# Linear attention and gated MLP on one core: one more tile pair of V as a Strassen group, and exps queued one product later

## The chip, the cores and the metric

One core of one Trainium2 chip runs the whole kernel. The metric is device time in microseconds; below, "us". The same program is run several times, and one further execution is recorded by the hardware profiler. All times inside the kernel are counted from the start of the profiled span.

## The reference

The input x has 2048 tokens of 1024 features, in bf16. Two blocks follow each other:

```
h  = x + A(layernorm(x))            # linear attention, 32 heads of 32
h2 = h + B(layernorm(h))            # gated MLP with 3584 hidden features

A:  q, k, v = split(x @ wqkv)
    phi(t) = where(t > 0, t + 1, exp(t)) + 1e-6
    kv = sum over tokens of phi(k) v ;  z = sum over tokens of phi(k)
    o  = phi(q) kv / (phi(q) z + 1e-6) ;  return o @ wo
B:  gate = x @ W_gate ; up = x @ W_up
    return (relu(gate) * up) @ W_down
```

The change concerns block A alone: the products that make k, v and q, the function phi, and the sum kv.

## The kernel before, in words

The 2048 tokens are 16 tiles of 128 ("st" 0 to 15). A tile is loaded, normalised by VectorE (DVE) with statistics from DVE (`ln1_stats`, L630 to L640) or from ScalarE (`ln1_stats_act`, L654 and L659, which ends on GpSimd, POOL), and turned over into `xnT`: the first four by TensorE (PE), the others by a DMA transpose that SP issues (`T1d`, L526). SP's queue is one list; behind each transpose stands the load of a later tile.

The instructions of all engines are written down in one order by the program, and each engine keeps its own part of that order. A planner adds the waits: an instruction waits for the last writer of what it reads, and for the readers of what it writes. So the place of a call in the source decides what stands ahead of it on its engine.

Two tiles form a pair p. The products of a pair with wk, wv or wq are made by `sgroup` (L833) in a form of Strassen's method, with seven products in place of eight. Each product is four matmuls of 512 columns. The order in a group, with the copies and additions between, is:

| step on PE | then |
|---|---|
| P1 into bank a | ACT copies a to bank b (fk1, L621) |
| P7 into bank f | ACT copies f to a buffer (s7, L621) |
| P6 onto b | ACT copies b to bank c (fk2, L621) |
| P2 onto a | a is the first result, "11" |
| P5 onto c | ACT copies c to a buffer (sc, L621); DVE adds f to it: result "22" |
| P4 onto b | DVE adds b to s7: result "21" |
| P3 onto c | c is the last result, "12" |

P6 needs fk1, P5 needs fk2, and P3, which writes c, needs sc to have read it. The buffer of sc is a single one, `btmp[0]`; s7 alternates between two (`atmp` and `btmp[1]`). The results 22 and 21 stand in these two buffers until they are used.

For k and q each result goes through phi: an exp on ACT (L684), and two instructions on DVE, a minimum and an addition (L688) and the final maximum (L691). I call the two "fin", the last alone "phi", and write exp22 and phi22 for those of result 22. The exp of 11 is issued in its own group. Those of 22, 21 and 12 are put into the table `pend` and issued in the next group (for q groups exp12 in its own); `hook(i)` issues what `pend[i]` holds and what the caller has asked for at that place. hook(1) comes after fk1, hook(2) after s7, hook(3) after fk2, hook(4) after P2 and its exp, hook(5) after sc and the addition, hook(6) after P4, hook(7) at the end.

For v the results are only copied: 11 and 12 by ACT (L970), 21 and 22 by DVE's addition (L964).

The order of the first stage: the v products of tiles 0 to 5 are plain, those of tiles 0 to 3 ahead of all groups (`v_piece`, eight matmuls for half of a tile, copied by ACT at L789); then the group k0, the pieces of v for tiles 4 and 5, and the groups k1, v3, k2, v4, k3, v5, k4, v6, k5, v7, k6, k7, and eight q groups, q0 to q3 (r = 0) and q4 to q7 (r = 1). `kvaccs(p)` adds a pair of tiles into kv with 16 small matmuls of 129 columns, eight for a tile. In the v groups it stands between P4 and P3 (hook 6). It first uses the even tile (results 11 and 12 of the k group), then the odd one (21, then 22). In q4 to q7 the same place holds `a2_num`, and DVE has the division `a2_div` besides (L1053, L1056, L1058).

`x_sums(p)` (L825, four DVE instructions) makes the sums of x that a group of pair p needs; they are used for k, v and q alike. `twk`, `twv` and `twq` are lists of DVE instructions that make the sums of the weights (L800); each pop issues one. `norms(p)` normalises the two tiles of pair p and issues their transposes. The k and v groups and q0 to q3 draw on five PSUM banks, q4 to q7 on four (`A_POOL`), the oldest first. After q7 comes the output product with wo (`a4_mm`, and `a4_h`, L1082), and then block B, which the change leaves alone.

Of the kernel before, what the change touches and what calls it, by code (L numbers as in the profile page):

```python
# [132 lines left out]
def bass_sequential_preLN__linear_attn_block__glu_gated_reglu__prompt_kernel(  # L133
# [64 lines left out]
    with es:  # L198
# [137 lines left out]
        def bank(b, w=512):  # L336
            return ps[:, b, 0:w]
# [375 lines left out]
        def ln1_stats(st):  # L713
            i = st % NX1
            ln1_k[st] = ln_stats(x1[:, i, :], B_x1[i], "ln1_%d" % st)
# [55 lines left out]
        def v_piece(st, h, mid=None):  # L771
            b = alloc_bank(P1_POOL)
            nt = ND2 + h
            for dc in range(NDC):
                if mid is not None and dc == NDC // 2:
                    mid()
                mm(bank(b, NW), xnT[:, dc, st * P:(st + 1) * P], wkv[:, dc, nt * NW:(nt + 1) * NW],
                   dc == 0, dc == NDC - 1, [xnT_buf(st, dc), B_wkv[nt][0 if dc < WKH else 1]], B_bank[b],
                   "v_%d_%d" % (st, h))
            v_copy(b, st, h)  # L780
# [32 lines left out]
        def x_sums(p):  # L813
            def xb(k, t):
                st = 2 * p + t
                return xnT[:, k * KH:(k + 1) * KH, st * P:(st + 1) * P]

            def s(i):
                return Sx(i)[:, :, p * P:(p + 1) * P]

            def bx(k, t):
                return [B_xnT[2 * p + t][k]]

            def add(i, in0, in1, op, reads):
                PL.add("dve", lambda e: e.tensor_tensor(out=s(i), in0=in0, in1=in1, op=op), reads=reads,  # L825
                       writes=[B_Sx[i][p]], name="Sx%d_%d" % (i + 1, p))

            add(2, xb(0, 0), xb(0, 1), ALU.subtract, bx(0, 0) + bx(0, 1))
            add(0, xb(0, 1), xb(1, 1), ALU.add, bx(0, 1) + bx(1, 1))
            add(1, s(0), xb(0, 0), ALU.subtract, [B_Sx[0][p]] + bx(0, 0))  # L830
            add(3, xb(1, 0), s(1), ALU.subtract, [B_Sx[1][p]] + bx(1, 0))

        def sgroup(pool, tok_major, X, SX, W, TW, e11, e12, e21, e22, name, hooks=(), isq=False):  # L833

            hooks = dict(hooks)

            def prod(b, x, w, start, nm):
                (xf, xr), (wf, wr) = x, w
                for kk in range(KH):
                    xa, wa = xf(kk), wf(kk)  # L840
                    l, r = (xa, wa) if tok_major else (wa, xa)
                    o = bank(b)
                    if len(r.shape) == 3:
                        o = o.rearrange("p (a b) -> p a b", b=r.shape[2])
                    mm(o, l, r, start and kk == 0, kk == KH - 1, xr + wr, B_bank[b], name + nm, skip=True)

            def hook(i):
                for f_ in pend.pop(i, ()):
                    f_()
                if i in hooks:  # L850
                    hooks[i]()

            a = alloc_bank(pool)
            f = alloc_bank(pool)
            b = alloc_bank(pool)
            prod(a, X(0, 0), W(0, 0), True, "P1")
            ident_act(bank(b), bank(a), [B_bank[a]], [B_bank[b]], name + "fk1")
            hook(1)
            prod(f, SX(2), TW(2), True, "P7")
            grp[0] += 1  # L860
            s7, b7 = [(atmp, B_at), (btmp[:, 1, :], B_bt[1])][grp[0] % 2]
            sc, bc = btmp[:, 0, :], B_bt[0]
            ident_act(s7, bank(f), [B_bank[f]], [b7], name + "s7")
            hook(2)
            c = alloc_bank(pool)
            prod(b, SX(1), TW(1), False, "P6")
            ident_act(bank(c), bank(b), [B_bank[b]], [B_bank[c]], name + "fk2")
            hook(3)
            prod(a, X(1, 0), W(1, 0), False, "P2")
            for f_ in e11(bank(a), B_bank[a]):  # L870
                f_()
            hook(4)
            prod(c, SX(0), TW(0), False, "P5")
            ident_act(sc, bank(c), [B_bank[c]], [bc], name + "sc")
            s22 = e22(bank(f), B_bank[f], sc, bc)
            s22[0]()
            hook(5)
            prod(b, X(1, 1), TW(3), False, "P4")
            s21 = e21(bank(b), B_bank[b], s7, b7)
            s21[0]()  # L880
            hook(6)
            prod(c, SX(3), W(1, 1), False, "P3")
            s12 = list(e12(bank(c), B_bank[c]))
            if isq:
                s12.pop(0)()
            pend[1] = s12
            pend[2] = list(s22[1:])
            pend[3] = list(s21[1:])
            hook(7)

        pend = {}
# [50 lines left out]
        def k_group(p, hooks=()):  # L942
            X, SX = x_ops(p)
            W, TW = w_ops(wkv, bw_k, tw_k, B_TWk)

            def dst(t, h):
                st = 2 * p + t
                return pk_ap(st)[:, h * NW:(h + 1) * NW], B_pk[pk_slot(st)][h]

            def pl(t, h):  # L950
                d, db = dst(t, h)
                return lambda b, bb: phi_steps(b, bb, d, db, "k_%d_%d" % (2 * p + t, h))
            sgroup(P1_POOL, True, X, SX, W, TW, pl(0, 0), pl(0, 1),
                   add_phi(*dst(1, 0), "k_%d_0" % (2 * p + 1)),
                   add_phi(*dst(1, 1), "k_%d_1" % (2 * p + 1)), "k%d" % p, hooks)
# [470 lines left out]
        twv = w_sums(wv_, bw_v, tw_v, B_TWv, "TWv", KH)  # L1426
# [10 lines left out]
        m5()  # L1437
        twk.pop(0)()
        v_piece(3, 0)
        q5()  # L1440
        ln1_stats(4)
        twk.pop(0)()
        v_piece(1, 1)
        ln1_norm(4)
# [7 lines left out]
        q6()  # L1452
        twv.pop(0)()
        twk.pop(0)()
        twv.pop(0)()
        v_piece(3, 1)
        for i in range(2):
            load_wq(i)
        NP_ = NST // 2

        def kv_hooks(p, nq):

            sq = []
            A, B = 2 * p + 6, 2 * p + 7

            def k1():
                if p > 0 and A < NST:
                    ln1_stats(A)
                for _ in range(nq[0]):
                    twq.pop(0)()  # L1470

            def k5():
                if B < NST:
                    m_, q_ = ln1_stats_act(B)
                    m_()
                    sq.append(q_)

            def k6():
                for f_ in sq:
                    f_()  # L1480
                if 3 <= p + 2 < NP_:
                    x_sums(p + 2)
            return {1: k1, 5: k5, 6: k6}

        def norms(p):
            for st in (2 * p, 2 * p + 1):
                if st < NST:
                    ln1_norm(st)
                    T1d(st)

        def kvaccs(p):
            kvacc(2 * p)
            kvacc(2 * p + 1)

        k_group(0, kv_hooks(0, (0, 0)))
        def run_pend(i):
            for f_ in pend.pop(i, ()):
                f_()

        v_piece(4, 0, lambda: run_pend(1))  # L1500
        run_pend(2)
        v_piece(4, 1, lambda: run_pend(3))
        x_sums(1)
        v_piece(5, 0)
        norms(3)
        twv.pop(0)()
        v_piece(5, 1)
        x_sums(2)
        kvaccs(0)
        NQ = {2: (0, 1), 3: (0, 1), 4: (0, 1), 5: (2, 2), 6: (1, 0)}  # L1510
        for p in range(1, NP_):
            nq = NQ.get(p, (0, 0))
            hooks = kv_hooks(p, nq)
            if p == NP_ - 1:
                hooks[5] = lambda h5=hooks[5]: (h5(), kvaccs(NP_ - 2))
            k_group(p, hooks)
            if p + 2 < NP_:
                def v6(p=p, nq=nq):
                    norms(p + 3)
                    kvaccs(p)  # L1520
                    for _ in range(nq[1]):
                        twq.pop(0)()
                v_group(p + 2, {6: v6})
# [4 lines left out]
        for r in range(2):  # L1528
            for ct in range(NG // 2):
                hooks = {}  # L1530
                if r == 0 and ct == 0:
                    hooks[6] = lambda: kvaccs(NP_ - 1)
                if r == 0 and ct == 2:
                    hooks[6] = kvfin
                if r == 1:
                    hooks[6] = lambda t=ct: a2_num(t)
                q_group(r, ct, hooks)
                if r == 1:
                    pend[1].insert(1 if ct + 1 < NG // 2 else 0, lambda t=ct: a2_div(t))
                if r == 0 and ct == 0:  # L1540
                    for i in range(TPP + NX2):
                        load_x2(i)
# [105 lines left out]
```

## Time and profile before

| | |
|---|---|
| median of 3 runs | 748.24 us (748.11 to 748.42) |
| profiled execution | 747.75 us |
| its span, first to last instruction | 746.0 us |
| granted TensorE clock | 0.999 |
| busy, PE / DVE / ACT / POOL | 736.1 / 536.7 / 309.7 / 43.9 us |
| PE's weight loads | 336.0 us |
| DMA moved | 113.38 MB |

The profiled execution took 1.75 us more than its span, and is 0.49 us under the median. A line of the timeline gives the start and the length of an instruction (or of several alike, "x4"), its engine, its line in the kernel, what it writes and reads, and in brackets the idle time of the engine just before it with what ended it. "PE" are matmuls and "PEld" the weight loads that go ahead of them; a weight load that is the first after a wait starts together with its matmul, others some 0.2 us earlier. The changed code runs between 9 and about 180 us. By stretches, the busy times of the engines are:

| stretch, us | PE | DVE | ACT |
|---|---|---|---|
| 24.0 to 37.3 (k0, v pieces) | 13.25 | 10.97 | 9.26 |
| 37.3 to 112.0 (k and v groups) | 73.88 | 59.49 | 49.08 |
| 112.0 to 145.0 (k7, q0 to q3) | 32.67 | 25.32 | 21.61 |
| 145.0 to 171.6 (q4 to q7) | 26.60 | 24.51 | 17.62 |

### The profile page before, as it was taken

To read this page: it belongs to the slowest core of one execution; us is meant where nothing else is said; L and a number is where in the kernel's file an instruction comes from. 1 tells how busy PE (TensorE), PEld (TensorE's weight loads), DVE (VectorE), ACT (ScalarE), POOL (GpSimd) and SP (SyncE) were. 2 spreads that over 40 slices of the span, in tenths; PEclk is the share of its full clock that TensorE was granted. 3 is DMA by queue.
4 is the path that set the end of the run, shared out by engine and by line. 5 is a ranking of instruction groups with operands and counts; after the bars stand their busy time and mean duration, and the time that the engine had idled before them with its cause. 6 is when DMAs were issued, how large, how long until landed. Compare 5 with 4: busy or idle time off the path is not lost.

```text
span 746.0 us, 10031 instructions
## 1 busy us (share of the span) xinstructions
PE 736.1 (99%) x3539; PEld 336.0 (45%) x3595; DVE 536.7 (72%) x1071; ACT 309.7 (42%) x536; POOL 43.9 (6%) x90
## 2 busy tenths in 40 slices
PE   9999999999999999999999999999999999999998
PEld 4444444344554444444444444444444444444443
DVE  7788866898775899787877585766867677563343
ACT  4767656665832354544543100035444454520000
POOL 2411000001350000000000010000000000000000
PEclk9999999999999999999999999999999999999999
DMA  9642144023998797666428899742324242036764
GB/s 305 202 103 68 35 135 156 1 29 84 230 223 248 222 278 210 179 176 171 142 85 253 231 254 305 240 121 77 110 61 112 58 113 56 1 85 184 211 189 135
DMA packets 160226, 113.38 MB, mean 152 GB/s; under 512 B 51505, under 2 KB 141361, under 8 KB 160177
## 3 DMA queue, kind: packets, MB, share of 16 engines
q1 hardware_dynamic: 160176, 112.75, 54.1%
q8 instruction: 28, 0.46, 0.3%
q14 instruction: 22, 0.17, 0.1%
HBM read 85.46 MB, written 15.73 MB: 136 GB/s over the span
## 4 chain that ended last, share of the span: by engine, by line
PE 88%; DVE 5%; ACT 4%; issue 2%; DMA 0%; SPq 0%; DVEq 0%; POOL 0%; ACTq 0%; POOLq 0%
PE ps L616 88%; DVE RAB L691 1%; ACT ps L621 1%; ACT RX L684 1%; DVE RE L1058 1%; DVE RX L688 1%; ACT RXH L654 1%; ACT RXH L659 1%; ACT RX L621 1%; DVE RX L903 0%; DMA RW<-in_B_W_down_dram 0%; SPq L522 0%; DVE RXH L1082 0%; PE ps L748 0%; DVE RE L691 0%
## 5 line engine op out<-in xcount | busy, mean ns | idle before, releaser
L621 ACT ACTIVATE ps<-ps 128x512 f32<-128x512 f32 x154 | 89.8, 584 | 180.2 <-PE ps L616 161.5
L616 PE MATMUL ps<-RC,RO 128*128 128x512 f16 x672 | 154.4, 379 | 0.5 <-DVE RE L1239 0.4
L616 PE MATMUL ps<-RW,RAB 128*128 128x512 f16 (+1 forms) x681 | 150.1, 379 | 0.6
L616 PEld LDWEIGHTS ps<-RW,RAB 128*128 128x128 bf16 (+1 forms) x692 | 67.7, 98 | 81.6
L616 PE MATMUL ps<-RH,RWG 128*128 128x512 bf16 x435 | 103.2, 379 | 1.0 <-DVE RAB L1232 0.3
L621 ACT ACTIVATE RE<-ps 128x512 f32<-128x512 f32 x120 | 70.8, 597 | 75.3 <-PE ps L616 52.8
L616 PEld LDWEIGHTS ps<-RC,RO 128*128 128x128 f16 x672 | 65.5, 98 | 80.5 <-ACT ps L621 1.1
L616 PE MATMUL ps<-RC,RWG 128*128 128x512 f16 x320 | 76.6, 379 | 0.1
L616 PEld LDWEIGHTS ps<-RH,RWG 128*128 128x128 bf16 x448 | 43.8, 98 | 53.4 <-DVE RAB L1232 0.8
L1232 DVE TENSOR_TENSOR RAB<-ps,RAB 128x512 bf16<-128x512 f32 x28 | 19.3, 690 | 63.6 <-PE ps L616 63.6
L621 ACT ACTIVATE RAB<-ps 128x512 bf16<-128x512 f32 x56 | 33.4, 597 | 61.9 <-PE ps L616 61.8
L616 PE MATMUL ps<-RH,RO 128*128 128x512 bf16 (+1 forms) x242 | 58.3, 379 | 0.7
L616 PE MATMUL ps<-RW,RE 128*128 128x512 bf16 x248 | 56.8, 379 | 0.8 <-DVE RXH L1082 0.4
L616 PE MATMUL ps<-RAB 128*128 128x512 bf16 x196 | 47.7, 379 | 0.3
L616 PEld LDWEIGHTS ps<-RC,RWG 128*128 128x128 bf16 (+1 forms) x320 | 30.0, 98 | 39.9 <-ACT ps L621 5.9
L1163 DVE TENSOR_TENSOR RO<-RWG,RO 128x512 f16<-128x512 bf16 x108 | 45.4, 420 | 1.8
L1163 DVE TENSOR_TENSOR RO<-RWG 128x512 f16<-128x512 bf16 x108 | 40.7, 418 | 3.2 <-DMA RWG<-in_B_W_up_dram 1.6
L1239 DVE TENSOR_TENSOR RE<-ps,RE 128x512 f32<-128x512 f32 x56 | 38.3, 690 | 4.9 <-ACT RE L621 4.9
L1244 DVE TENSOR_TENSOR RE<-ps,RE 128x512 f32<-128x512 f32 x56 | 38.1, 681 | 0.0
L616 PEld LDWEIGHTS ps<-RH,RO 128*128 128x128 f16 (+1 forms) x256 | 24.6, 98 | 29.4 <-ACT RX L621 1.1
L616 PEld LDWEIGHTS ps<-RW,RE 128*128 128x128 bf16 x256 | 24.5, 98 | 27.9 <-DVE RXH L1082 0.7
L688 DVE TENSOR_SCALAR RX<-RX 128x512 bf16<-128x512 bf16 x64 | 18.6, 290 | 22.8 <-ACT RX L684 22.7
(118 smaller groups left out, 764.8 us busy)
## 6 DMA issues: line engine op xcount, KB each, us to landing
RWG<-in_B_W_gate_dram SPq DMA_DIRECT2D x28, 512.0 KB, 4.0
RWG<-in_B_W_up_dram SPq DMA_DIRECT2D x28, 512.0 KB, 5.1
RW<-t_scr SPq DMA_DIRECT2D x56, 256.0 KB, 3.3
RW<-in_B_W_down_dram SPq DMA_DIRECT2D x42, 256.0 KB, 4.0
RW<-in_B_W_down_dram SPq DMA_DIRECT2D x14, 512.0 KB, 4.1
t_scr<-RW SPq DMA_DIRECT2D x14, 512.0 KB, 5.0
RE<-in_A_x_dram SPq DMA_DIRECT2D x23, 256.0 KB, 3.2
RAB<-in_A_wqkv_dram SPq DMA_DIRECT2D x8, 512.0 KB, 8.0
```

Source lines behind the costliest of these rows:

```text
L616: lambda e: e.matmul(out_ap, lhsT, rhs, start=start, stop=stop, skip_group_check=skip),
L621: PL.add("act", lambda e: e.activation(out=dst, in_=src, func=func), reads=reads, writes=writes, name=name)
L654: PL.add("act", lambda e: e.activation(out=junk, in_=src, func=ACTF.Identity, scale=1.0 / D, accum_out=sv[:, 0:1]), reads=src_bufs, writes ...
L659: PL.add("act", lambda e: e.activation(out=junk, in_=src, func=ACTF.Square, scale=float(D) ** -0.5, accum_out=sv[:, 1:2]), reads=src_bufs, ...
L684: PL.add("act", lambda e: e.activation(out=Et[:, k, :], in_=src, func=ACTF.Exp), reads=[src_buf], writes=[B_E[k]], name=name + "_exp")
L688: PL.add("dve", lambda e: e.tensor_scalar(out=Et[:, k, :], in0=Et[:, k, :], scalar1=1.0, scalar2=1e-6, op0=ALU.min, op1=ALU.add), reads=[] ...
L691: PL.add("dve", lambda e: e.scalar_tensor_tensor(out=dst_ap, in0=src, scalar=C1, in1=Et[:, k, :], op0=ALU.add, op1=ALU.max), reads=[src_bu ...
L1058: PL.add("dve", lambda e: e.tensor_tensor(out=osb[:, k, :].rearrange("p (g h e) -> p g h e", h=HPG, e=Dh), in0=nv[:, :, 0:P].rearrange("p ...
L1163: PL.add(eng, lambda e: e.tensor_tensor(out=Tring[:, k, j], in0=in0, in1=in1, op=ALU.subtract), reads=reads, writes=[B_T[k][j]], name="T%d ...
L1232: PL.add("dve", lambda e: e.tensor_tensor(out=hh[:, f1, 0:SBW], in0=bank(BA[1]), in1=r11[:, rr, :], op=ALU.mult), reads=[B_bank[BA[1]], B_ ...
L1239: PL.add("dve", lambda e, w=w: e.tensor_tensor(out=ftmp[:, 4 + w, :], in0=bank(BF_[w]), in1=ftmp[:, 2 + w, :], op=ALU.add), reads=[B_bank[ ...
L1244: PL.add("dve", lambda e, w=w: e.tensor_tensor(out=ftmp[:, 6 + w, :], in0=bank(BB[w]), in1=ftmp[:, w, :], op=ALU.add), reads=[B_bank[BB[w] ...
```

## The change

It does four things. The v products of tiles 4 and 5 (pair 2) are made by a group, v2, instead of four plain pieces. For that the loop over pairs starts at 0, `x_sums(2)` moves into k0 (hook 6), `x_sums(1)` and `norms(3)` into v2, and the last of the `twv` instructions ahead of k0. In every group that has exps pending from the group before, exp22 with its fin goes from hook(2) to hook(3), so behind fk2, and exp21 with its fin from hook(3) to hook(4), so behind P2 and exp11. The sums kv of the pairs 6 and 7 go to the end of k7 (from the place behind P5) and to the end of q0 (from the place behind P4). And the DVE statistics of tile 4, with the POOL instruction that ends them, go ahead of `q5()`, the second half of the ACT statistics of tile 5. Since there is one group more, s7 of each later group uses the other of its two buffers.

```diff
@@ sgroup
             pend[1] = s12
-            pend[2] = list(s22[1:])
-            pend[3] = list(s21[1:])
+            pend[3] = list(s22[1:])
+            pend[4] = list(s21[1:])
             hook(7)
@@ first stage
         v_piece(3, 0)
+        ln1_stats(4)
         q5()
-        ln1_stats(4)
         twk.pop(0)()
...
         twv.pop(0)()
+        twv.pop(0)()
         v_piece(3, 1)
@@ kv_hooks
-                if 3 <= p + 2 < NP_:
+                if p + 2 < NP_:
                     x_sums(p + 2)
@@ loop over pairs
-        k_group(0, kv_hooks(0, (0, 0)))
-        def run_pend(i):
-            for f_ in pend.pop(i, ()):
-                f_()
-
-        v_piece(4, 0, lambda: run_pend(1))
-        run_pend(2)
-        v_piece(4, 1, lambda: run_pend(3))
-        x_sums(1)
-        v_piece(5, 0)
-        norms(3)
-        twv.pop(0)()
-        v_piece(5, 1)
-        x_sums(2)
-        kvaccs(0)
         NQ = {2: (0, 1), 3: (0, 1), 4: (0, 1), 5: (2, 2), 6: (1, 0)}
-        for p in range(1, NP_):
+        for p in range(NP_):
             nq = NQ.get(p, (0, 0))
             hooks = kv_hooks(p, nq)
             if p == NP_ - 1:
-                hooks[5] = lambda h5=hooks[5]: (h5(), kvaccs(NP_ - 2))
+                hooks[7] = lambda: kvaccs(NP_ - 2)
             k_group(p, hooks)
             if p + 2 < NP_:
                 def v6(p=p, nq=nq):
+                    if p == 0:
+                        x_sums(1)
                     norms(p + 3)
                     kvaccs(p)
@@ q groups
                 if r == 0 and ct == 0:
-                    hooks[6] = lambda: kvaccs(NP_ - 1)
+                    hooks[7] = lambda: kvaccs(NP_ - 1)
```

## The prediction

> **What bounds the kernel now.** I read first the page's busy times and chain, then the waits of PE's weight loads, then the timeline of single groups between 23 and 172 us, where the changed code runs.
>
> ```profile
> PE 88%; DVE 5%; ACT 4%; issue 2%; DMA 0%; SPq 0%; DVEq 0%; POOL 0%; ACTq 0%; POOLq 0%
> ```
> ```profile
> PEld ps L616 <- ACT ps L621: 18.8, 44, 0.7
> PEld ps L616 <- ACT RX L621: 3.7, 10, 0.4
> ```
>
> TensorE bounds the kernel, so only what shortens or delays its stream counts. Its weight loads wait mostly for copies on ACT: "ps L621" is fk1 or fk2, "RX L621" is sc. Most of such a wait is normal: a load that runs ahead shows idle too. So I measure by starts of products (four matmuls each). Unhindered ones follow at 0.865 us (P1 to P7 at 70.64 and 71.50), hence 0.216 us a matmul and 6.06 us a group of 28.
>
> The group q1, in the timeline (start, duration, engine):
>
> ```profile
> 128.04 0.60 ACT L621 ACTIVATE RX<-ps 128x512 f32<-128x512 f32 x1 [0.28 <-PE ps L616]
> 128.54 0.62 ACT L684 ACTIVATE RX<-RX 128x512 bf16<-128x512 f32 x1
> 129.06 0.59 ACT L621 ACTIVATE ps<-ps 128x512 f32<-128x512 f32 x1
> 129.52 0.69 DVE L691 SCALAR_TENSOR_TENSOR RAB<-RX 128x512 bf16<-128x512 f32 x1
> 129.57 0.61 ACT L684 ACTIVATE RX<-RXH 128x512 bf16<-128x512 f32 x1
> 129.70 0.55 PEld L616 LDWEIGHTS ps<-RWG,RH 128*128 128x128 f16 x4 [0.48 <-ACT ps L621]
> 130.09 0.59 ACT L684 ACTIVATE RX<-ps 128x512 bf16<-128x512 f32 x1
> 130.82 0.60 ACT L621 ACTIVATE RX<-ps 128x512 f32<-128x512 f32 x1 [0.15 <-issue]
> 131.47 0.55 PEld L616 LDWEIGHTS ps<-RH,RO 128*128 128x128 bf16 x4 [0.37 <-ACT RX L621]
> ```
>
> On ACT stand s7, exp22 of the group before, fk2, exp21, this group's exp11, sc. P5's load at 129.70 waited for fk2. P6 had started at 127.82, and results can be read 1.04+0.09 us after such a start (sc starts at 130.82 after P5 at 129.70), so fk2 could have run at 128.95; exp22 held it 0.11 us. In the k groups, where no exps are pending, P5 starts 1.77 us after P6 (66.20 to 67.97); here 1.88, in v4 2.00 (72.46 to 74.46). So the exps cost about **0.12 us in each of q1 to q7 and 0.23 in v3 to v7, k7 and q0**.
>
> [...] fk2 followed exp22 0.52 us after its start, though its data were there. [...]
>
> **The change, part by part.**
>
> *v pieces to a group.* From the first piece of tile 4 (29.49) to k1 (37.34) PE takes 7.85 us: 32 matmuls (6.92) and kvacc. A v group with kvacc takes 7.36 (v4 at 70.64 to k3 at 78.00). So **-0.49**; four matmuls fewer are 0.86, and 0.37 comes back as the group's waits. ACT gets six copies for four and DVE two additions, inside those 7.36.
>
> *The fourth twv earlier, ln1_stats(4) before q5().* The twv is one 1.22 us addition on DVE. DVE had waited 1.64 us at 21.67 for POOL's rstd of tile 4, which stood behind q5's POOL work; moved ahead, it is ready by about 19.5, and tile 5's norm starts near 21.07 instead of 22.13. The 1.06 won pays for the twv (1.13 start to start): DVE is free at 27.3 as before, when exp11 of k0 ends at 27.66. Both transposes issue some 1.6 us earlier on SP. **0**; without that cover at most +1.1.
>
> *x_sums(1) and norms(3).* DVE now does, in v2, phi21, two additions, x_sums(1) (1.67), then the norms of tiles 6 and 7. From v4's row moved by 41.15 us, x_sums(1) starts near 36.95 and norm 6 ends at 39.17; before it ended at 36.57. SP issues transpose, x load, transpose: the second is 1.91 us after the first (36.59 to 38.50), so at 41.1, and transposes land 3.1 to 3.7 us after issue: 44.4. x_sums(3) in k1 wants it at 37.03 + 6.50 = 43.53 (k2 started at 64.45, its x_sums at 70.95). P7 of v3 then starts near 44.9 instead of 44.1: **+0.8** (0 to 1.2). Later pairs have 6.5 us from issue to use and keep their slack.
>
> *exps one product later.* The copies fk2 gain the 0.12 and 0.23 above. But exp22, fin22 and exp21, fin21 all move, and three things stand behind them:
>
> (a) **sc waits for phi22.** sc writes btmp[0], which phi22 of the group before still reads. exp22's start to phi22's end takes 1.67 us (128.54 to 130.21). In q1 fk2 goes to 128.95, exp22 to 129.46, phi22 ends at 131.13. P5 (now 129.59, 0.64 after fk2) would let sc start at 130.72; exp11 and exp21 on ACT hold it to 130.99, phi22 to 131.16. P3 follows 0.65 later: 131.81 instead of 131.47. **+0.34 in q1, q2, q3 = +1.02.** q0 loses its cover too, as kvaccs(7) moves behind P3: P5 0.23 earlier, P3 0.49 held: **+0.26**. In k7 kvaccs(6), which had stalled 0.26 us for phi21, moves to the end: P3 held to 116.95, next group at 118.76 against 118.77: **0**.
>
> (b) **kvacc waits for phi21 in the v groups.** Its second eight matmuls need it:
>
> ```profile
> 74.33 0.62 ACT L684 ACTIVATE RX<-RXH 128x512 bf16<-128x512 f32 x1
> 75.31 0.69 DVE L691 SCALAR_TENSOR_TENSOR RE<-RXH,RX 128x512 bf16<-128x512 f32 x1
> 75.99 1.13 PEld L616 LDWEIGHTS ps<-RE 128*128 128x128 bf16 x16
> ```
>
> phi21 ended at 76.00; kvacc began on PE at 76.20 and takes 0.94 us (124.26 to 125.20 in q0), so its second half began at 76.67. Afterwards, exp22 starts at 74.10, the v copy at 74.61, exp21 at 75.11; phi22 ends at 75.77 and phi21 at 76.80. PE, 0.23 earlier, wants it at 76.44: 0.41 of wait. **+0.18 in each of six v groups = +1.08.** sc itself is covered by kvacc there.
>
> (c) **DVE is full in q5 to q7.** One fin12 to the next is 6.71 us (159.25 to 165.96) without a gap: four fins 0.93 each, a2_div 1.75, two additions 1.25.
>
> ```profile
> 160.79 1.22 DVE L1058 TENSOR_TENSOR RE<-ps,rden 128x1024 bf16<-128x1024 f32 x1
> 161.93 0.28 DVE L688 TENSOR_SCALAR RX<-RX 128x512 bf16<-128x512 bf16 x1
> 162.86 0.29 DVE L688 TENSOR_SCALAR RX<-RX 128x512 bf16<-128x512 bf16 x1
> 163.79 0.28 DVE L688 TENSOR_SCALAR RX<-RX 128x512 bf16<-128x512 bf16 x1
> ```
>
> With only four banks fk1 writes the bank that the last addition (add21) reads. From the end of add21: fk1 +0.03, P6 +0.65, fk2 +1.13, exp22 +0.51, fin22 +0.64: 2.96 us, in which DVE has 0.93 + 1.75 = 2.68 of work. Then three fins and the additions, 4.06: a period of 7.02. Starting with q4's late phi22, P3 of q7 is 0.72 late and DVE's additions 1.37. The output stage begins DVE-bound: a4_mm(2) at 180.24 waited 0.39 for a4_h(0). So DVE's lateness counts: **+1.37**, of which PE's own is 0.72 (0 if DVE finds its gaps elsewhere).
>
> s7's buffers change parity with one group more, and both alternate on: 0. Bytes, SP's order and later stages stay; those are PE-paced, so the delay stays to the end.
>
> **Sum:** -0.49 + 0.8 + 1.02 + 0.26 + 1.08 + 1.37 = **+4.0 us**. The profiled execution took 747.75 (span 746.0, 1.75 around it) and would become 751.8; the median, 748.24, lies 0.49 above it: I say **752.2**.
>
> **Rivals.**
>
> 1. *Faster: the waits go and nothing takes their place.* Gains: 5 x 0.23 + 2 x 0.23 + 7 x 0.12 = 2.45, with the 0.49: 745.3. For it: the 0.48 waits are plain in the rows. It decides at one place: if phi22 ends before P5's result can be copied. In q1 it is 131.13 against 130.72, so the 1.67 us would have to shrink by 0.41; nothing shortens it, and ACT alone (exp11, exp21) already holds sc by 0.27. 12%.
>
> 2. *Smaller loss.* The transposes land in time and q4 to q7 don't build up: 4.0 - 0.8 - 1.37 = +1.9, 750.1. Against it: DVE's rows are gapless. Its lower half, if kvacc's wait is milder too (-1.1), is no change. 18%.
>
> 3. *Heavier.* fk1 of one group and sc of the next feed each other in r = 0 too, and the transposes land at 44.8: +6, 754.2. 8%.
>
> 4. *My case*: 62%, 750.7 to 753.5. That the change doesn't move the exps is out: the instruction order of the changed kernel has fk2 ahead of exp22 and sc behind exp21, waiting on DVE.
>
> A measurement of this kernel tells about 0.2%, 1.5 us. Faster is rival 1, 0.12; same is the lower part of rival 2, 0.08; slower 0.80. The range, 748.6 to 754.0, leaves out rival 1 and the upper part of rival 3.
>
> **What would show it.** Right: P5 1.77 us after P6 in v and q groups; in q1 to q3 P3 over 2.1 us after P5, its load waiting for ACT RX, sc for DVE; kvacc in two runs of eight; q5 to q7 some 7.0 us apart; P7 of v3 waiting for DVE. Wrong: P3 1.77 after P5 in q1 to q3, or q groups under 6.25 us; then rival 1 holds.

## The result: 753.51 us against 748.17, and the profile after

The changed kernel takes 753.51 us (median, 753.23 to 753.82), the kernel before 748.17 in the same measurement: a ratio of 1.0071 with an interval of 1.0054 to 1.0089. It is slower, by 5.3 us where +4.0 was predicted; the profiled execution took 753.38 us (span 751.6). The chain of the changed kernel, and what its weight loads waited for between 23 and 178 us (us in total, times, longest):

```profile
PE 82%; DVE 9%; ACT 3%; issue 3%; DMA 2%; SPq 1%; POOL 0%; DVEq 0%; ACTq 0%
```
```profile
PEld ps L616 <- ACT ps L621: 16.0, 41, 0.7
PEld ps L616 <- ACT RX L621: 6.6, 12, 0.8
PEld ps L616 <- DVE RWG L825: 4.4, 6, 1.5
PEld ps L616 <- DVE RE L691: 2.4, 6, 0.4
PEld ps L616 <- DVE RX L903: 1.7, 4, 0.4
```

The kernel before, over the same stretch (sc, 3.7 us, as in the prediction's lines):

```profile
PEld ps L616 <- ACT ps L621: 17.8, 42, 0.6
PEld ps L616 <- DVE RWG L825: 1.4, 5, 0.3
PEld ps L616 <- DVE RE L691: 0.3, 1, 0.3
```

The copies fk1 and fk2 ("ps L621") are waited for less, 16.0 us where the kernel before had 17.8. Everything below has grown: sc ("RX L621") from 3.7, the sums of x (L825) from 1.4, phi21 (L691, into RE) from 0.3, and DVE's addition add21 (L903) is new. One wait was exchanged for four.

The group q1 of the changed kernel, in the timeline (start, duration, engine):

```profile
131.79 0.58 ACT L621 ACTIVATE ps<-ps 128x512 f32<-128x512 f32 x1 [0.31 <-PE ps L616]
132.28 0.62 ACT L684 ACTIVATE RX<-RX 128x512 bf16<-128x512 f32 x1
132.42 0.55 PEld L616 LDWEIGHTS ps<-RWG,RH 128*128 128x128 f16 x4 [0.36 <-ACT ps L621]
132.80 0.59 ACT L684 ACTIVATE RX<-ps 128x512 bf16<-128x512 f32 x1
133.26 0.69 DVE L691 SCALAR_TENSOR_TENSOR RAB<-RX 128x512 bf16<-128x512 f32 x1
133.28 0.63 ACT L684 ACTIVATE RX<-RX 128x512 bf16<-128x512 f32 x1
133.99 0.60 ACT L621 ACTIVATE RX<-ps 128x512 f32<-128x512 f32 x1
134.64 0.33 PEld L616 LDWEIGHTS ps<-RH,RO 128*128 128x128 bf16 x3 [0.81 <-ACT RX L621]
```

fk2 (131.79) now goes ahead of exp22 (132.28), and P5 starts at 132.42, 1.77 us after P6 at 130.65: the gain is there. Then ACT has exp11 (132.80) and exp21 (133.28), phi22 ends on DVE at 133.95, and only then sc runs, at 133.99; P3 starts at 134.64, 2.22 us after P5 instead of 1.77.

The profiled execution adds up as follows. Groups are taken from start of P1 to start of P1 of the next; "predicted" joins the terms of the prediction that fall into a group.

| stretch | before | after | measured | predicted |
|---|---|---|---|---|
| start, until v of pair 2 | 29.49 | 29.13 | -0.36 | 0 |
| v of pair 2 (pieces, v2) | 7.85 | 8.17 | +0.32 | -0.49 + 0.18 |
| v3 | 7.36 | 8.65 | +1.29 | +0.8 + 0.18 |
| v5 | 7.36 | 8.15 | +0.79 | +0.18 |
| v4, v6, v7 | 7.36, 7.36, 7.28 | 7.54, 7.54, 7.46 | +0.54 | +0.54 |
| k7, q0 to q3 | 33.77 | 34.98 | +1.21 | +1.28 |
| q4 to q7 | 6.71 each | 7.01 each | +1.20 | +0.72 |
| start of the output stage | | | +0.63 | +0.65 |
| sum | | | +5.62 | +4.04 |

The two profiled executions differ by 5.63 us. The first row is no effect: up to 16 us the kernels run the same program, and their plain v products begin anywhere from 16.12 to 16.81 us. Without it the changes cost 6.0.

Two of the waits in the rows of the changed kernel: P7 of v3 for the sums of x (L825), and, in v4, the second eight matmuls of kvacc for phi21 (L691):

```profile
45.57 1.69 PE L616 MATMUL ps<-RW,RWG 128*128 128x512 f16 x7 [1.06 <-DVE RWG L825]
63.46 0.67 PEld L616 LDWEIGHTS ps<-RE 128*128 128x128 bf16 x8
64.53 0.47 PEld L616 LDWEIGHTS ps<-RE 128*128 128x128 bf16 x8 [0.41 <-DVE RE L691]
```

### The profile page after: what moved, and what is told of

It reads as the page before. It is cut to its first block, busy times and chain, and to the rows that moved or that the text cites. A ratio compares the mean times of both kernels' runs of the same rounds, so it can differ in the third digit from the quotient of the medians.

```text
span 751.6 us, 10032 instructions
## 1 busy us (share of the span) xinstructions
PE 735.5 (98%) x3535; PEld 334.1 (44%) x3591; DVE 537.3 (71%) x1073; ACT 312.0 (42%) x538; POOL 44.2 (6%) x90
## 4 chain that ended last, share of the span: by engine, by line
PE 82%; DVE 9%; ACT 3%; issue 3%; DMA 2%; SPq 1%; POOL 0%; DVEq 0%; ACTq 0%
PE ps L616 82%; ACT ps L621 2%; DVE RAB L691 2%; DVE RX L688 1%; DVE RE L691 1%; DMA RAB<-RXH 1%; ACT RX L684 1%; DMA RE<-in_A_x_dram 1%; DVE RX L903 1%; SPq L522 1%; DVE RW L800 1%; DVE st L630 0%; DMA RW<-in_B_W_down_dram 0%; DVE RC L800 0%; ACT RX L621 0%
## 5 line engine op out<-in xcount | busy, mean ns | idle before, releaser
L621 ACT ACTIVATE ps<-ps 128x512 f32<-128x512 f32 x156 | 90.7, 582 | 190.0 <-PE ps L616 165.1
L621 ACT ACTIVATE RE<-ps 128x512 f32<-128x512 f32 x120 | 70.8, 597 | 74.8 <-PE ps L616 52.6
L621 ACT ACTIVATE RAB<-ps 128x512 bf16<-128x512 f32 x56 | 33.4, 597 | 61.4 <-PE ps L616 61.4
L616 PE MATMUL ps<-RAB 128*128 128x512 bf16 x172 | 42.5, 379 | 0.3
```

The source lines that it names most:

```text
L616: lambda e: e.matmul(out_ap, lhsT, rhs, start=start, stop=stop, skip_group_check=skip),
L621: PL.add("act", lambda e: e.activation(out=dst, in_=src, func=func), reads=reads, writes=writes, name=name)
```

## The experiments

All ratios are to the kernel before, run on the same chip. Kernels "after with ..." are the changed kernel with one edit.

### The two halves alone

The exps alone, put into the kernel before:

```diff
-            pend[2] = list(s22[1:])
-            pend[3] = list(s21[1:])
+            pend[3] = list(s22[1:])
+            pend[4] = list(s21[1:])
...
-        run_pend(2)
-        v_piece(4, 1, lambda: run_pend(3))
+        run_pend(3)
+        v_piece(4, 1, lambda: run_pend(4))
...
-                hooks[5] = lambda h5=hooks[5]: (h5(), kvaccs(NP_ - 2))
+                hooks[7] = lambda: kvaccs(NP_ - 2)
...
-                    hooks[6] = lambda: kvaccs(NP_ - 1)
+                    hooks[7] = lambda: kvaccs(NP_ - 1)
```

> The kernel before with the exps one product later and the sums kv of pairs 6 and 7 at the ends of k7 and q0; tiles 4 and 5 stay plain pieces. Theory (sc behind phi22 and exp21, kvacc behind phi21, DVE's loop in q4 to q7): v3 to v7 +0.18 each, q0 +0.28, q1 to q3 +0.32 each, q4 to q7 +0.30 each, the start of the output stage +0.6, in all about +4.0: 752.2 us. Rival (the loss sits in the start, with v2 and the transposes): +1 at most, 749.2.

751.68 us against 747.66: 1.0053 (1.0041 to 1.0066), +4.0. v3 to v6 take 7.53, q2 and q3 6.62, q4 to q7 7.01 to 7.02. The exps cost what their own rows say, without v2.

The group v2 alone, with the exps and the kvaccs at their old places:

```diff
-            pend[3] = list(s22[1:])
-            pend[4] = list(s21[1:])
+            pend[2] = list(s22[1:])
+            pend[3] = list(s21[1:])
...
-                hooks[7] = lambda: kvaccs(NP_ - 2)
+                hooks[5] = lambda h5=hooks[5]: (h5(), kvaccs(NP_ - 2))
...
-                    hooks[7] = lambda: kvaccs(NP_ - 1)
+                    hooks[6] = lambda: kvaccs(NP_ - 1)
```

> The changed kernel with the exps back at hooks 2 and 3 and the sums kv of pairs 6 and 7 at their old places; v2, the earlier twv and ln1_stats(4) stay. Theory: four matmuls less and v2's waits give -0.5, x_sums(2) late +0.5, the transposes for x_sums(3) late +1.1: about +1.1 to the kernel before, 749.3 us. Rival: +4, 752.2.

749.13 us: 1.0018 (1.0012 to 1.0025), +1.5. v3 takes 8.24, v5 8.15. The two halves add up to 5.5, the change itself to 5.3 to 5.6: they hardly interact. v2 itself takes 7.86, as long as the pieces with their four matmuls more; the loss lies in v3 and v5, behind the instructions that were moved for it.

### The exps: three waits, one edit each

After with two buffers for sc, so that sc need not wait for phi22 (a second buffer, alternating by group; to make room, the small temporaries of the division `a2_div` shrink from four buffers to one, and the line numbers rise by 2):

```diff
-            sc, bc = btmp[:, 0, :], B_bt[0]
+            sc, bc = [(btmp[:, 0, :], B_bt[0]), (btm2[:], B_b2)][grp[0] % 2]
```

> The changed kernel with two buffers for sc, used in turn, so that sc doesn't wait for phi22 (small scratch of the division goes from four buffers to one for the room). If both phi22 and the order on ACT hold sc: P3 of k7 and q0 to q3 starts 0.12 us earlier only, as exp21 stands ahead of sc still, about -0.6 in all: 752.9 us. If phi22 alone held it: P3 0.43 earlier in each of five groups, -2: 751.4. If the buffer played no part: 753.5.

752.84 us, 1.0067 (1.0053 to 1.0081): 0.3 us less than the change by the ratios, too little for these intervals, but the groups show it. q1 to q3 take 6.42 to 6.43, where the changed kernel has 6.62 and the kernel before 6.29 to 6.34; q4 gives 0.2 back (7.23 for 7.02). The timeline of q1 with two buffers:

```profile
132.68 0.69 DVE L693 SCALAR_TENSOR_TENSOR RAB<-btm,RX 128x512 bf16<-128x512 f32 x1
132.69 0.63 ACT L686 ACTIVATE RX<-RX 128x512 bf16<-128x512 f32 x1
133.21 0.60 ACT L623 ACTIVATE RX<-ps 128x512 f32<-128x512 f32 x1
133.86 0.55 PEld L618 LDWEIGHTS ps<-RH,RO 128*128 128x128 bf16 x4 [0.61 <-ACT RX L623]
```

sc runs at 133.21, right behind exp21 and before phi22 has ended (133.37). P3 is 2.03 us after P5 (131.83), between the 2.22 of the change and the 1.77 of before: 0.13 of the 0.32 us that q1 and q2 had lost stays. sc now follows exp21 on ACT without a gap, so what is left stands there, on exp11 and exp21. As the prediction had it, two things hold sc.

After with the exps that pend into q groups at their old places:

```diff
-            pend[3] = list(s22[1:])
-            pend[4] = list(s21[1:])
+            pend[2 if isq else 3] = list(s22[1:])
+            pend[3 if isq else 4] = list(s21[1:])
```

> The changed kernel with the exps pending from q groups back at hooks 2 and 3 (those from k groups stay late). Theory: q1 to q3 6.29 us again (-0.95), q4 to q7 6.71 again (-1.2), the output stage no longer late by DVE (-0.6): -2.8, 750.7 us. Rival (only the start matters): 753.3.

750.77 us, 1.0037 (1.0025 to 1.005). q1 to q3 and q4 to q7 are back at their times of before, and a4_mm(2) no longer starts late. It stands 3.0 over before where the change stands 5.3: (a) in q1 to q3 and (c) make about half of the loss.

After with another order in kvacc: for odd tiles the eight small matmuls take result 22 first and 21 last:

```diff
-            for g in range(NG):
+            for g in (range(NG) if st % 2 == 0 else (4, 5, 6, 7, 0, 1, 2, 3)):
```

> The changed kernel with the eight kv matmuls of the odd tile in the order of result 22 first, then 21. If phi21 is what PE waits for in the v groups: the wait falls from about 0.41 us by the time of four small matmuls, 0.23, in each of six v groups: -1.4, 752.1 us. If phi22 or the copies of v were waited for: no gain, 753.5.

752.02 us, 1.0054 (1.0042 to 1.0067). v4 and v6 take 7.30 us, less than the 7.36 of before. So phi21 was what kvacc waited for, and with that wait gone the later exps do gain 0.06 us in a v group. Not all of the 1.3 us by which its ratio lies under the change's is that, though: v5 takes 7.30 too, where the changed kernel has 8.15, and that is a transpose that landed earlier (below).

### The group v2: who is late for P7, and what the sums of the weights cost

After with norms(3) ahead of x_sums(1) in v2:

```diff
-                    if p == 0:
-                        x_sums(1)
                     norms(p + 3)
+                    if p == 0:
+                        x_sums(1)
```

> The changed kernel with norms(3) ahead of x_sums(1) in v2: transposes of tiles 6 and 7 issue 1.6 us earlier, x_sums(1) ends 1.0 later. If the order of these on DVE makes v3's wait: P7 of v3 without wait (-1.1), P7 of k1 waits 0.3, net -0.8: 752.7 us. If the transposes are slow for another reason: no gain, 753.5.

752.73 us, 1.0067 (1.0055 to 1.008). v3 falls from 8.65 to 7.53: the late transpose of tile 7 was the cause. x_sums(1) is now 0.21 late for k1.

The wait of v2 itself was not predicted. The timelines of the changed kernel, PE:

```profile
29.13 1.03 PE L616 MATMUL ps<-RAB 128*128 128x512 bf16 x4
30.72 1.91 PE L616 MATMUL ps<-RW,RWG 128*128 128x512 f16 x8 [0.56 <-DVE RWG L825]
```

and DVE with POOL, ahead of it:

```profile
18.59 1.23 DVE L800 TENSOR_TENSOR RC<-RAB 128x2048 f16<-128x2048 bf16 x1
18.72 1.50 POOL L640 TENSOR_TENSOR rstd<-rstd,neghalf 128x1 f32<-128x1 f32 x1 [6.20 <-DVE rstd L637]
20.33 0.55 DVE L673 TENSOR_SCALAR RXH<-RE,mv,rstd 128x1024 bf16<-128x1024 bf16 x1 [0.51 <-POOL rstd L640]
21.86 0.55 DVE L733 TENSOR_SCALAR RXH<-RE,s 128x1024 bf16<-128x1024 bf16 x1 [0.99 <-POOL s L668]
```

In the kernel before:

```profile
21.00 0.56 POOL L640 TENSOR_TENSOR rstd<-rstd,neghalf 128x1 f32<-128x1 f32 x1
22.13 0.54 DVE L733 TENSOR_SCALAR RXH<-RE,s 128x1024 bf16<-128x1024 bf16 x1
```

P7 of v2 waits 0.56 us for x_sums(2). POOL's rstd of tile 4, 0.56 us long in the kernel before (at 21.00), takes 1.50 here, and DVE's sum of two weight blocks (L800) runs beside it from 18.59, where in the kernel before DVE stood idle beside it. rstd begins 0.13 us after the addition and ends 0.40 us after it (20.22 and 19.82). So norm 4 starts at 20.33 and not at 19.5. Norm 5 (L733) then waits 0.99 us more, for the s of tile 5 on POOL (L668, 21.27 to 21.83), which now stands behind rstd. It starts at 21.86 where 21.07 was predicted; before it started at 22.13, in an execution whose plain v products began 0.36 us later (16.48 against 16.12). Of the predicted cover of 1.06 us nothing is left.

Two edits test it. After with that sum behind the norms of tiles 4 and 5:

```diff
         q5()
-        twk.pop(0)()
         v_piece(1, 1)
         ln1_norm(4)
         T1d(4)
         ln1_norm(5)
         T1d(5)
+        twk.pop(0)()
```

> The changed kernel with the second twk addition behind the norms of tiles 4 and 5 instead of ahead. If POOL's rstd of tile 4 (1.50 us there, 0.55 elsewhere) is stretched by DVE's addition of two SBUF operands running beside it: rstd takes 0.55, norm 4 starts near 19.4 instead of 20.3, DVE is through with its sums about 1 us earlier, P7 of v2 doesn't wait (0.5): 753.0 us. If the stretch has another cause: rstd stays at 1.5 and the time at 753.5.

754.43 us, 1.0091 (1.0075 to 1.0106): a miss. Its timeline, POOL and DVE:

```profile
18.98 0.55 POOL L640 TENSOR_TENSOR rstd<-rstd,neghalf 128x1 f32<-128x1 f32 x1 [6.15 <-DVE rstd L637]
19.64 0.55 DVE L673 TENSOR_SCALAR RXH<-RE,mv,rstd 128x1024 bf16<-128x1024 bf16 x1 [0.73 <-POOL rstd L640]
21.17 0.55 DVE L733 TENSOR_SCALAR RXH<-RE,s 128x1024 bf16<-128x1024 bf16 x1 [0.98 <-POOL s L668]
```

rstd is back at 0.55 with DVE idle beside it, so the addition beside it was what had made it 1.50. Norm 5 starts at 21.17, in an execution that began 0.32 us later (16.44 against 16.12), so 1.0 us earlier: the cover is there. But the addition, which had run in DVE's waits, now stands behind them: DVE waits 0.73 and 0.98 us for POOL with nothing to do, and P7 of v2 waits 0.81.

After with the fourth twv addition behind x_sums(2), at the end of k0, instead of ahead of k0:

```diff
-        twv.pop(0)()
         twv.pop(0)()
         v_piece(3, 1)
...
+            if p == 0:
+                hooks[7] = lambda: twv.pop(0)()
             k_group(p, hooks)
```

> The changed kernel, with the fourth twv addition issued at the end of k0 (behind x_sums(2)) instead of ahead of k0. Theory: in the changed kernel the four weight sums in a row, one of them stretching POOL's rstd, hold DVE until 28.1 us, and x_sums(2) comes 0.56 us late for P7 of v2. With the addition behind x_sums(2) these sums come 1.1 us earlier, P7 of v2 no longer waits for DVE, and v2 takes 7.6 instead of 8.17 us: 0.5 us less than the changed kernel, about 753.0 us, ratio to before about 1.0065; nothing else moves. Rival: the place of the twv costs nothing and P7 is late for another reason (the additions of k0, the bank), then v2 keeps its 8.17 and the ratio stays at 1.0071.

753.18 us against 747.68, 1.0072 (1.0058 to 1.0086). The median shows no gain. The profile does: v2 takes 7.53 us (29.74 to 37.27), and the wait for L825 is gone from it. That is 0.32 under the 7.85 of the pieces, where the prediction had 0.31 for the group with kvacc's wait. The profiled execution started its v products 0.61 us later than that of the changed kernel (16.73 and 16.12), which hides the 0.64 in it; the medians can't tell 0.5 us with intervals this wide.

### v5: a transpose that lands late

v5 lost 0.79 us and not 0.18. (Each landing below is read from the one profiled execution of its kernel.) In the changed kernel its sums of x waited for the second transpose of v4, that of tile 11, issued at 68.05. What the trace answers on its landing, before and after:

```profile
L526 SPq DMA_TRANSPOSE RAB<-RXH x1: 1241/1241/1241, 66.3 to 66.3; - x1
DMA to landing us min/median/max: 3.5/3.5/3.5
```
```profile
L526 SPq DMA_TRANSPOSE RAB<-RXH x1: 1231/1231/1231, 68.1 to 68.1; - x1
DMA to landing us min/median/max: 5.1/5.1/5.1
```

The DMA queues tell what differs: in the changed kernel an instruction fetch of 16 KB lies between 68 and 71 us, at 69.7, 1.6 us behind that transpose; before, it came at 64.1, 2.2 us ahead of it. The line of queue 8 of the changed kernel (packets, MB, share):

```profile
q8 instruction: 1, 0.02, 1.9%
```

In all ten kernels that had v2 and that were run so far, this transpose landed after 4.1 to 5.7 us; in the two without v2 it landed after 3.5. The DMA queues of six show the place of the fetch. In four with v2 it followed the transpose: by 0.6 to 0.7 us with the exps early in q groups, with the late twv and in the last version (landings 5.0, 4.9 and 4.7), by 1.6 in the changed kernel (5.1). In the two without v2 it was 2.2 and 2.3 us ahead. After 4.1 us the transpose still came in time (v5 of the version with the other order in kvacc). To see whether the fetch is the cause, I set out to move it: the 12 idle matmuls of 512 columns that open the kernel became 24 of 256, the same columns and 24 instructions more for TensorE; its next work starts at 6.3 us with both.

```diff
-        pe_dummies(12, P1_POOL)
+        pe_dummies(24, P1_POOL, 256)
```

> The changed kernel, with the 12 idle matmuls of 512 columns at the start replaced by 24 of 256: same work for TensorE, 24 instructions more ahead of everything else. Theory: the second transpose for v5 lands 5.1 us after its issue because an instruction fetch of 16 KB (queue 8) at 69.7 falls 1.6 us behind its issue at 68.05; if that queue feeds TensorE, 24 instructions more bring the fetch about 2.2 us forward, to 67.5, ahead of that transpose, as in the kernel before (fetch 2.2 us ahead, landing after 3.5 us). Then v5 takes 7.54 like v4 and v6 instead of 8.15, and the run is 0.6 us shorter, 752.9 or 1.0063. Rival 1: the fetch isn't TensorE's, so it stays where it is, and v5 too (1.0071). Rival 2: the fetch moves and the transpose still lands after 5 us: then the fetch is not the cause.

756.04 us, 1.0108 (1.0091 to 1.0125). At v5 the time is the theory's: tile 11's transpose lands after 3.5 us, and v5 takes 7.54. That the queue feeds TensorE was an assumption, and the 2.2 us were an estimate; the rows of this kernel show neither. At v3 tile 7's transpose landed after 5.6 us instead of 4.0:

```profile
L526 SPq DMA_TRANSPOSE RAB<-RXH x1: 1232/1232/1232, 41.4 to 41.4; - x1
DMA to landing us min/median/max: 5.6/5.6/5.6
```
```profile
43.84 1.03 PE L616 MATMUL ps<-RAB 128*128 128x512 bf16 x4
47.55 2.84 PE L616 MATMUL ps<-RW,RWG 128*128 128x512 f16 x8 [2.68 <-DVE RWG L825]
50.18 1.82 PE L616 MATMUL ps<-RAB 128*128 128x512 bf16 x4
51.84 1.03 PE L616 MATMUL ps<-RW,RWG 128*128 128x512 f16 x4
```

PE stood 2.68 us idle, and its products then took up to twice as long until 51.8: the four matmuls at 50.18 took 1.82 us, four at 43.84 had taken 1.03, and the granted clock was 0.66 from 47.5 to 50.2 and 0.51 from there to 51.8. v3 takes 11.76 us, 3.1 more than in the changed kernel. The sum was a miss, by a loss at another place. Where the fetch lies with the 24 idle matmuls is shown for the last version below. (k0 also took 0.6 us longer: its fk1 stood on ACT behind the statistics of tile 6, whose load came late; why it came late wasn't tested. v2 takes 7.54 there.)

### All repairs together

After with the exps early in q groups, kvacc's order, norms(3) ahead of x_sums(1), and the weight sum behind the norms of tiles 4 and 5, each as shown above:

> The changed kernel with four edits at once: exps from q groups at hooks 2 and 3, the order 22 then 21 for the odd tile, norms(3) ahead of x_sums(1), the second twk behind the norms of tiles 4 and 5. If the parts add up: -2.8 -1.4 -0.8 -0.5 = -5.5, 748.0 us, level with the kernel before; if they cover one another, above 749.

748.51 us against 747.81, 1.0011 (1.0003 to 1.0019). v4 to v6 take 7.30 to 7.32 and q4 to q7 6.71, but P7 of v2 still waits, k1 takes 6.64 since x_sums(1) is late, and q0 still has the late exps.

The last version therefore takes kvacc's order and the late twv, has the exps early also from k7 into q0 with kvaccs(7) behind P4 again, and splits x_sums(1): its first two instructions go to hook 2 of v2, where DVE had stood idle for 1.03 us, the other two behind norms(3).

```diff
-            pend[3] = list(s22[1:])
-            pend[4] = list(s21[1:])
+            pend[2 if isq or name == "k7" else 3] = list(s22[1:])
+            pend[3 if isq or name == "k7" else 4] = list(s21[1:])
...
-                    if p == 0:
-                        x_sums(1)
                     norms(p + 3)
+                    if p == 0:
+                        x_sums(1, (1,))
...
-                v_group(p + 2, {6: v6})
+                v_group(p + 2, {6: v6, 2: lambda: x_sums(1, (0,))} if p == 0 else {6: v6})
```

> The group v2 kept, and every wait that the study found taken away: exps of q groups (and of k7) pending into the next group at their old places, kvaccs(7) behind P4 of q0 again, result 22 first in kvacc of odd tiles, the fourth twv behind x_sums(2), and x_sums(1) split: its first two instructions at hook 2 of v2, where DVE stood idle for 1.0 us, the other two behind norms(3). exps in k and v groups stay one product later. Theory: v2 7.6 us, v3 to v6 7.30, k1 6.19, k7 with q0 14.8, q1 to q7 as before: 1.2 us less than the version with the first three of these repairs (748.51, which was 0.7 over before), so about 747.3 where before takes 747.8, ratio 0.9993. Rival: the sums in v2 push phi22 and phi21 later, so that kvacc and norms(3) wait again: v2 8.0, v3 7.7, ratio 1.0005.

747.68 us against 747.68, 0.9999 (0.9991 to 1.0007): no difference. k1 takes 6.19, v3, v4 and v6 7.30, the q groups their times of before. But v2 takes 7.75, since a load of kvacc waits 0.62 us for phi21 there (the rival's effect, in v2 alone), and v5 takes 7.81: tile 11's transpose is issued at 66.33, to a hundredth the time of before, and lands after 4.7 us instead of 3.5, with the fetch 0.6 us behind it and not 2.2 ahead. Fewer matmuls and shorter waits bring some 0.3 us, and this takes 0.45.

The same version with the 24 idle matmuls:

> The version with the waits taken away (747.68 where before took 747.68), with the same 24 idle matmuls. There the fetch at 66.9 followed the second transpose for v5 at 66.33 by 0.6 us, it landed after 4.7 us, and v5 took 7.81 instead of 7.30. Theory: the fetch moves to about 64.7, the landing to 3.5, v5 to 7.30, the whole to 747.2, ratio 0.9993; at v3 the fetch moves to about 41.6, 2.2 us behind the transpose of tile 7, which may give 0.2 of it back. Rival: v5 keeps 7.81 and the ratio stays at 1.0000.

748.53 us, 1.0012 (1.0003 to 1.002). Again v5 falls, to 7.30 (tile 11's transpose, issued at 68.40, lands after 3.5, and the fetch, at 65.9, is 2.5 us ahead of it), and v3 rises, from 7.30 to 8.57, by far more than the 0.2 that was expected. The landing of tile 7's transpose in these two versions, without and with the idle matmuls:

```profile
L526 SPq DMA_TRANSPOSE RAB<-RXH x1: 1231/1231/1231, 39.4 to 39.4; - x1
DMA to landing us min/median/max: 3.4/3.4/3.4
```
```profile
L526 SPq DMA_TRANSPOSE RAB<-RXH x1: 1231/1231/1231, 40.2 to 40.2; - x1
DMA to landing us min/median/max: 5.5/5.5/5.5
```

With the idle matmuls a fetch of 16 KB lies at about 43.0, 2.8 us behind this transpose (issued at 40.16) and before its landing at 45.7. No version run here beats the kernel before by more than a measurement tells.

## Why the prediction was right, and where its sum was not

The direction, the mechanism and most of the terms held; the time of 752.2 was 1.3 us short, within the range. Four terms were too small: v2 by 0.63 us, v3 by 0.31, v5 by 0.61, q4 to q7 with the output stage by 0.46. In the profiled executions 0.36 of these 2.0 us is hidden by the earlier start. An estimate with all of them, 748.24 + 6.0, is 754.2, just outside the range, so that the time fell inside is in part luck.

- **fk2 ahead of exp22** gave what was read from the rows: P5 1.77 us after P6 in the q groups. The gain never reached the end of a group, as one copy later the same ACT queue and phi22 held sc. *(a)*: +0.32, +0.33 and +0.28 in q1 to q3 against 0.34, +0.27 in q0 against 0.26, nothing in k7. With two buffers 0.2 of it went in each group.
- *(b)* kvacc waiting for phi21: +0.18 in v4, v6 and v7, exactly the prediction's; kvacc runs in two runs of eight, the second load waiting 0.40 us for L691. Taking 22 first removed it.
- *(c)* The loop q4 to q7 has the predicted period:

```profile
158.71 1.22 DVE L1058 TENSOR_TENSOR RE<-ps,rden 128x1024 bf16<-128x1024 f32 x1
160.21 0.29 DVE L688 TENSOR_SCALAR RX<-RX 128x512 bf16<-128x512 bf16 x1 [0.27 <-ACT RX L684]
165.73 1.23 DVE L1058 TENSOR_TENSOR RE<-ps,rden 128x1024 bf16<-128x1024 f32 x1
167.22 0.29 DVE L688 TENSOR_SCALAR RX<-RX 128x512 bf16<-128x512 bf16 x1 [0.27 <-ACT RX L684]
```

  DVE divides 7.02 us after it divided, and waits 0.27 us for exp22: the prediction's 2.96 less 2.68. But it let the loop take hold from q5 on. It holds from q4: four groups lose 0.30 each, 1.20 by the end of q7 where 0.72 was put, and then the output stage begins 0.63 late. That term was 1.37 and measured 1.83.
- *v pieces to a group*: -0.49 less the 0.18 of kvacc was right for the group alone (7.53 in the version with the late twv). **The step that failed is the twv at "0".** Its cover was to be 1.06 us of DVE's wait for POOL. None of it came: rstd took 1.50 us where the prediction had its length without an addition beside it, and the s of tile 5, which the prediction left out, then stood behind it on POOL, so that norm 5 started at 21.86 and not at 21.07. The sums of x for v2 started at 30.25; with the late twv they started at 30.07 in an execution that began 0.61 later, so 0.8 us earlier. P7 of v2 waited: +0.64, within the "at most +1.1" that the prediction named and did not take.
- *x_sums(1) and norms(3)*: +0.8 was +1.1 (v3 less kvacc's 0.18). The issue was at 41.07 as predicted (41.1), the landing at 45.1 and not 44.4: 4.0 us, above the 3.7 that the trace of before had shown as the longest.
- *"Later pairs keep their slack"* failed in v5, for +0.6. Nothing in the changed code lies there; a fetch came to lie behind a transpose. The last version shows landing and fetch move together: 4.7 us with the fetch 0.6 behind, 3.5 with it 2.5 ahead. Why it moved by 3.8 us against the transpose stays open: TensorE has four matmuls and four weight loads fewer, which is 0.9 us.

Rival 1 (faster) fell at the place named for it: phi22 ends 133.95, and P5's result could have been copied at 133.55 (1.13 after 132.42). Rival 3's time, 754.2, was near. Of its two parts one came true, the transpose that lands late (45.1; it had 44.8); the other, the feedback in r = 0, did not: q1 to q3 stay at 6.62.

## What to carry to other kernels

Moving an instruction behind the one that waits helps only if nothing later on the same queue, or on the buffer that it reads, is then the last to come: follow the moved instruction to the next use of its input and of its output before counting the gain. When a step is said to be covered by another engine's latency, take that engine's time under the load that will then run beside it: here POOL's 0.56 us became 1.50. And where transposes have a slack of a microsecond or less, a change in the number of TensorE's instructions far ahead of them can use it up, at a place the diff doesn't touch (here 24 more at the start moved landings by 1.2 to 2.1 us); look for it before blaming the edit.

## What the runs showed of the hardware

- In the first stage (up to 100 us) a DMA transpose of one of these tiles (128x1024) landed 3.0 to 3.8 us after its issue, except for tile 7's and tile 11's in some kernels. Tile 11's landed after 5.1 us in the changed kernel, with a 16 KB instruction fetch 1.6 us behind its issue, and after 3.5 in the kernel before, with that fetch 2.2 us ahead. Two pairs of kernels that differ only in 24 instructions at the start moved the landings in both directions: tile 11's from 5.1 to 3.5 and from 4.7 to 3.5, tile 7's from 4.0 to 5.6 and from 3.4 to 5.5. In the second pair the fetch was 0.6 us behind tile 11's transpose at 4.7 and 2.5 ahead at 3.5; at tile 7's 5.5 one was about 2.8 us behind, with an 8 KB one (queue 14) in the same stretch, 42 to 44 us. A smaller fetch (8 KB, queue 14) 2.7 us behind tile 7's transpose went with 4.0 us in the changed kernel; that was not moved, and stays a correlation. How a fetch would delay a transpose was not shown.
- POOL's power on a 128x1 column (rstd, L640) took 0.56 us in the kernel before and 0.55 with the sum behind the norms, with DVE idle beside it, and 1.50 in the changed kernel, with a two-input DVE addition of 2048 columns beside it.
- In one execution, after 2.68 us of idle, TensorE was granted 0.66 of its clock from 47.5 to 50.2 us, 0.51 to 51.8, and 1.00 again after that. Its single weight loads follow one another at 0.43 us from 48.91 to 51.47. From the 0.66 over 2.7 us, an estimate is that it ran at full clock to 48.4 and at half for 3.4 us. The windows of the kernel with 24 idle matmuls (stretch and its length; busy times of PE, PEld, DVE, ACT and POOL, with numbers of instructions; then the granted clock, the DMA share and GB/s):

```profile
44.00:47.50 3.50, 0.87 (x5) 0.19 (x2) 0.67 (x3) 2.13 (x4) 1.06 (x3) 1.00 0.41 116
47.50:50.20 2.70, 2.65 (x9) 1.01 (x10) 2.08 (x5) 0.60 (x1) 0.00 (x0) 0.66 0.00 0
50.20:51.80 1.60, 1.60 (x5) 0.59 (x4) 0.17 (x1) 1.12 (x2) 0.00 (x0) 0.51 0.00 0
51.80:54.70 2.90, 2.83 (x25) 1.68 (x24) 2.30 (x5) 1.60 (x3) 0.00 (x0) 1.00 0.00 0
```

  Waits of 1.06 us (the changed kernel, up to 45.57) and 1.20 us (the last version with 24 idle matmuls, up to 46.15) stand in v3 of other kernels: the granted clock was 1.00 in the first from 44.4 to 50.0, and 1.00 in the mean of the whole execution in the second.
